# Moving zero writes, table arithmetic, one weight pass and a weight load inside an attention and mixture-of-experts kernel

## Chip, cores and metric

The kernel runs on one core of one Trainium2 chip. The metric is the device time of one execution in microseconds (us). Three runs of the kernel before took 637.21, 634.17 and 636.15 us, a median of 636.15 us. The profiled execution took 632.04 us.

## What is computed

The reference has two halves. The first is linear attention with a decay for each head, over 4 batches, 8 heads, 768 positions and a head width of 64:

```
state = gamma * state + k[t] (outer) v[t]
y[t]  = q[t] @ state / sqrt(64)          gamma[h] = 1 - 2**(-5 - h)
```

The 8 heads of a position are joined to one row of 512, which gives 3072 rows x. The second half is a mixture of 8 experts with noise on the gate:

```
l = x @ w_gate + log(1 + exp(x @ w_noise)) * noise
the two largest l of a row pick two experts; their softmax gives two weights
out[row] = sum over the two of  weight * relu(x @ w1[e]) @ w2[e]
```

w1[e] is 512 x 1024 and w2[e] is 1024 x 512.

## The kernel before, in words

**Attention.** The 3072 positions are cut into 24 chunks of 128, six for each batch. A loop over j = 0 to 23 handles one chunk a turn, written out in full (no loop on the chip). All orders inside a turn are fixed by the program text: every engine works its own instructions in that order. In turn j TensorE does the score products of chunk j + 1 (`qk`, L365), the output from within the chunk (`y_in`, L378), two tiny products for the sum of squares (`x_total`, L407), the output from the carried state (L386), the new state (L396), the transposes of chunk j - 2 (`x_rows`, L422) and its gate products (`logits`, L435 and L438). GpSimd scales the queries two chunks ahead (`q_scale`, L346) and the values one chunk ahead (`v_scale`, L340). VectorE applies the mask and splits rows into an f16 part and its remainder (`x_lo`, L416); ScalarE forms the f16 part (`x_hi`, L412), squares, copies the state and copies transposed rows out. The attention rows are written to a buffer in device memory, xbuf (`x_store`, L428).

**The SP queue.** SyncE (SP) issues nearly all plain DMAs, in program order: the loads of chunk j + 4, the row store, weight loads (`w_load`, L187), the writes of zeros to the two output tensors (`zero_out`, L307, 512 KB each), and DMA transposes (`x_t`, L705 to L709). The output must be zero before the experts' results are added to it.

**Side work in the loop.** Four tables hold what else is done in a turn: `ahead_of`, `between`, `todo` (filled by `at`) and `late`. They place the router (`route_a` to `route_f`), the preparation of expert 0's weights, and the zero writes. Weights are split into f16 parts: ScalarE forms the first (`w_hi`), then the f32 weights are scaled (`w_scaled`: L228 on GpSimd, L226 on ScalarE) and GpSimd subtracts (`w_rest`, L232).

**The table.** For each batch the router makes a product of one-hot matrices (`table`, L584) whose result LST lists, for each expert and lane, the row that it serves. `route_f` (L589, L591) adds the batches up in `acc`, a tile in SBUF. `rows_of` (L599 to L602) turns it into row numbers `idx`, replacing empty places by a padding row. With these GpSimd gathers rows by indirect DMA (`gather`, L687), and `x_t` transposes them on the way into the tile `xe`. `pR` and `pL` are two PSUM banks that the router uses as scratch.

**Experts.** Expert 0 is started while the last batch is still being routed: its products (`mm1`, L824 to L826, and `mm2`, L1001 to L1003) are cut into units that `early` places between router steps. Experts 1 to 7 run in a loop. Each has a first product `mm1s` (L900 to L902) of 28 steps; a `hook` is called after each step s and places side work. Then up to seven blocks of 128 rows follow, each a second product into one of two PSUM banks (`pO`), emptied by ScalarE (`scaled`, L971) and added to the output by indirect DMA from GpSimd (`put`, L977). Beside the blocks VectorE and ScalarE prepare the next expert: `prepare` splits its first weights, and `x_sums` (L850 to L858) reads its transposed rows `xe`. `ahead(e + 1, ...)` asks for a block's rows: a gather on GpSimd, then a transpose on SP. `w_load(e + 1, "2", ...)` loads its second weights, 2 MB in two DMAs, into the only staging tile; it waits until `w_lo` (L220) has read the old ones, the last time in step 12.

Of the kernel before, what the change touches and what calls it, by code (L numbers as in the profile page):

```python
# [40 lines left out]
NCOL = NBLK * E  # L41
# [54 lines left out]
def moe_kernel(ctx, tc, qT, kT, kt, vt, noise, wgn, w1, w2, ctab, qtab, xbuf, gbuf, out):  # L96
# [22 lines left out]
    def K(n):  # L119
        return ct[:, _C[n][0]:_C[n][1]]  # L120
# [37 lines left out]
    wide = pR[:, 144:144 + NC * NL].rearrange("p (c e) -> p c e", c=NC)  # L158
    small = pR[:, 208:208 + 48]
    second_best = pR[:, 256:256 + NC]  # L160

    def pow2(ss, target, up, down=None):

# [423 lines left out]
    def route_f(b):  # L587
        if b == 0:
            nc.vector.tensor_copy(acc, LST)  # L589
        else:  # L590
            nc.vector.tensor_tensor(acc, acc, LST, op=OP.add)  # L591

    tk = consts.tile([128, NCOL], F32, name="tk")

    def rows_of(tk, n0, n1):

        padv = work.tile([128, NCOL], F32, name="padv")
        neg = work.tile([128, NCOL], F32, name="neg")
        nc.vector.tensor_scalar(padv[:, n0:n1], tk[:, n0:n1], 0.0, K("pad"), op0=OP.is_equal, op1=OP.mult)  # L599
        nc.vector.tensor_scalar(neg[:, n0:n1], tk[:, n0:n1], 0.0, float(TOK), op0=OP.is_lt, op1=OP.mult)  # L600
        nc.vector.tensor_tensor(neg[:, n0:n1], neg[:, n0:n1], padv[:, n0:n1], op=OP.add)
        nc.vector.scalar_tensor_tensor(idx[:, n0:n1], tk[:, n0:n1], 127.0, neg[:, n0:n1], op0=OP.add, op1=OP.add)  # L602

    def ranks():

        nc.vector.tensor_copy(cum, cump)
        m = E - 2
        n, s3, s4 = R["cum"][:, 2:E], [128, m, m], [128, m, NBLK, m]
        key = hp.tile([128, m], F32, name="key")
        nc.vector.scalar_tensor_tensor(key, n, 8.0, K("tie")[:, :m], op0=OP.mult, op1=OP.add)  # L610
        cm = hp.tile(s3, F32, name="cm")
        nc.vector.tensor_tensor(cm, key[:, None, :].to_broadcast(s3), key[:, :, None].to_broadcast(s3), op=OP.is_gt)
        rk = hp.tile([128, m], F32, name="rk")
        nc.vector.tensor_reduce(rk, cm, axis=AX.X, op=OP.add)
        pm = R["pm"] = hp.tile(s3, F32, name="pm")
        nc.vector.tensor_tensor(pm, rk[:, None, :].to_broadcast(s3),
                                K("i64")[:, :m, None].to_broadcast(s3), op=OP.is_equal)
        nc.vector.tensor_tensor(cm, pm, K("lidx")[:, None, 2:E].to_broadcast(s3), op=OP.mult)
        nc.vector.tensor_reduce(rk, cm, axis=AX.X, op=OP.add)
        nc.vector.tensor_copy(eid[:, :m], rk)  # L620
        tp = hp.tile(s4, F32, name="tp")
        v = acc[:, 2 * NBLK:].rearrange("p (e t) -> p t e", e=m)
        nc.vector.tensor_tensor(tp, v[:, None].to_broadcast(s4), pm[:, :, None, :].to_broadcast(s4), op=OP.mult)
        nc.vector.tensor_reduce(tk[:, 2 * NBLK:].rearrange("p (r t) -> p r t", r=m), tp, axis=AX.X, op=OP.add)
        rows_of(tk, 2 * NBLK, NCOL)
        nc.vector.tensor_tensor(cm, pm, K("rcap")[:, 1:, None].to_broadcast(s3), op=OP.mult)
        nc.vector.memset(capd, float(CAP))
        nc.vector.tensor_reduce(capd[:, 2:E], cm.rearrange("p r e -> p e r"), axis=AX.X, op=OP.add)
# [84 lines left out]
    for b in range(B - 1):  # L713
# [9 lines left out]
            late.setdefault(n + 8, []).append((route_f, (b,)))  # L723
        if b == B0 - 1:

            late[n + 8].append((rows_of, (acc, 0, 3)))
            for t in range(3):
                ahead_of.setdefault(n + 9, []).append((gather, 0, t, 0, 128, B0 * S))
                at(n + 10, x_t, 0, t)
# [8 lines left out]
    for i in range(4):  # L738
        at(3 + i, w_load, 0, "1", i)
        at(5 + i, w_sum, 0, "1", i)  # L740
        at(10 + i, w_hi, 0, "1", i)
        between.setdefault((11, 13, 16, 18)[i], []).append((w_scaled, nc.gpsimd, 0, "1", i))
        between.setdefault((12, 14, 17, 19)[i], []).append((w_rest, 0, "1", i))
        at(8 + i, w_load, 0, "2", i)
        at(14 + i, w_sum, 0, "2", i)
        at(19 + i, w_hi, 0, "2", i)
    at(23, w_scaled, nc.scalar, 0, "2", 0)
    at(22, w_load, 1, "1", 0, 2)
    at(22, w_load, 1, "1", 2, 2)
    for i in range(8):  # L750
        at((7, 11, 12, 13, 14, 15, 16, 17)[i], zero_out, i)
    for i in range(2):
        at(10, zero_out, 12 + i)
    for j, a in ((4, (lanes16, K("lanes"))), (4, (blks16, K("blks"))), (5, (lanes.bitcast(F32), lanes16.bitcast(F32))),
# [13 lines left out]
    for j in range(NCH):  # L768
# [27 lines left out]
        y_mm(j)  # L796
        if j >= 2:
            x_rows(j - 2)
            logits(j - 2)
        slip()  # L800
        for f, a in todo.get(j, []):
            f(*a)
# [253 lines left out]
    x_rows(NCH - 1)  # L1056
    logits(NCH - 1)
    x_store(NCH - 1)
    table(b - 1)
    route_f(b - 1)  # L1060
    rows_of(acc, 3, mid + 1)
    for t in range(3, mid + 1):
        gather(0, t, 0, min(128, SECOND - t * 128), (B - 1) * S)
    for t in range(3, mid + 1):
# [32 lines left out]
    early(1)  # L1097
    table(b)
    route_f(b)
    rows_of(acc, mid, 2 * NBLK)  # L1100
    for t in range(mid, NBLK):
        gather(0, t, SECOND - t * 128 if t == mid else 0)
    for t in range(mid, NBLK):
# [91 lines left out]
    for e in range(1, E):  # L1195
        more = e + 1 < E

        def hook(s):
# [11 lines left out]
            if s == (22 if e == 1 else 11):  # L1210
                out_scale(e, 0, len(blocks(e)))
            if more:
                if 2 <= s < 9:
                    ahead(e + 1, ((6, 0, 3, 1, 4, 2, 5)[s - 2],))
                if s in (14, 16, 18, 20):
                    w_sum(e + 1, "1", s // 2 - 7)
                if s == 26:
                    w_scale(e + 1, "1")

        mm1s(e, hook)  # L1220
        for n, t in enumerate(blocks(e)):
            if more:
                if n == 0:
                    w_load(e + 1, "2", 0, 2)
                    w_load(e + 1, "2", 2, 2)
                if n < 3:
                    prepare(e + 1, n)
                if n == 2:
# [123 lines left out]
```

## Time and profile before

| what | value |
| --- | --- |
| median of three runs | 636.15 us |
| profiled execution, own time | 632.04 us |
| its span, first to last instruction | 630.3 us |
| mean granted TensorE clock | 0.996 |
| TensorE busy (matmul) | 611.6 us, 97% |
| VectorE busy | 451.2 us, 72% |
| ScalarE busy | 391.8 us, 62% |
| GpSimd busy | 395.2 us, 63% |
| moved by DMA | 112.90 MB, mean 179 GB/s |

The table is to be read by stages, since an average over the span hides where an engine stands still. Attention ends near 115 us, expert 0 is in work until about 188 us, and the loop over experts 1 to 7 runs to about 620 us. Names in the profile: PE is TensorE, PEld its weight load, DVE VectorE, ACT ScalarE, POOL GpSimd, SP SyncE; L12 is a line of the kernel. `a <- b` says that a was written from b, or that a waited for b.

### The profile page before, as it was taken

What the parts mean: (1) busy time and instruction counts of PE and PEld (TensorE: products, weight loads), DVE (VectorE), ACT (ScalarE), POOL (GpSimd) and SP (SyncE); (2) the same over time, 40 slices, a digit from 0 to 9 for tenths busy, and PEclk for the clock granted to TensorE, in tenths of its full rate; (3) what the DMA queues carried; (4) which work ended last, traced back from release to release, by engine and by line L of the source; (5) the groups of instructions that cost most, each with busy time, mean ns of one, the idle gap of its engine ahead of it and who ended that gap; (6) DMA issues with size and microseconds to landing.
All of it is one profiled execution on the core that took longest, in us unless ns stands there. A gap on an engine that the chain in (4) does not pass through costs nothing.

```text
span 630.3 us, 13242 instructions
## 1 busy us (share of the span) xinstructions
PE 611.6 (97%) x5133; PEld 384.9 (61%) x5133; DVE 451.2 (72%) x952; ACT 391.8 (62%) x655; POOL 395.2 (63%) x278
## 2 busy tenths in 40 slices
PE   8999988999999999999999999999999999999995
PEld 5899877756755545554565446544654565445784
DVE  5679888788697795579657964796579557957720
ACT  4788877944456856586558655865586558556311
POOL 2657889525776885863687558657845674574154
PEclk9999999999999999999999999999999999999998
DMA  9999999867972597479546974787499549642043
GB/s 332 350 404 405 355 384 317 244 222 208 195 193 36 85 258 226 55 133 243 161 49 118 197 229 56 169 201 176 46 146 216 160 54 162 192 52 35 9 52 44
DMA packets 104321, 112.90 MB, mean 179 GB/s; under 512 B 64512, under 2 KB 78080, under 8 KB 100672
## 3 DMA queue, kind: packets, MB, share of 16 engines
q1 hardware_dynamic: 83296, 84.70, 45.5%
q0 software_dynamic: 20528, 26.90, 27.3%
q8 instruction: 41, 0.67, 0.4%
q10 hardware_dynamic: 432, 0.43, 0.2%
q14 instruction: 24, 0.20, 0.1%
HBM read 72.16 MB, written 26.47 MB: 156 GB/s over the span
## 4 chain that ended last, share of the span: by engine, by line
PE 83%; DVE 8%; DMA 3%; ACT 2%; issue 1%; POOL 1%; SPq 1%; POOLq 0%; ACTq 0%; DVEq 0%
PE pO L1001 11%; PE pO L1002 11%; PE pO L1003 11%; PE pH L900 11%; PE pH L902 10%; PE pH L901 10%; PE pA L365 2%; DVE am L372 2%; PE pY L378 2%; PE pO L992 2%; PE pT L1016 2%; PE pO L990 1%; PE pO L991 1%; PE pH L824 1%; DMA in_q<-qT 1%; PE pH L826 1%
## 5 line engine op out<-in xcount | busy, mean ns | idle before, releaser
L977 POOL DMA_INDIRECT out<-ot,idx x108 | 196.1, 1816 | 139.3 <-ACT ot L971 47.8
L1002 PE MATMUL pO<-w2l,h 128*128 128x512 f16 x336 | 127.3, 379 | 0.0
L1003 PE MATMUL pO<-w2h,h 128*128 128x512 f16 x336 | 127.3, 379 | 0.0
L1001 PE MATMUL pO<-w2h,h 128*128 128x512 f16 x336 | 127.3, 379 | 0.0
L924 DVE TENSOR_TENSOR s<-pH,s 128x416 f32<-128x416 f32 (+2 forms) x84 | 47.3, 571 | 45.0 <-PE pH L902 36.7
L697 POOL DMA_INDIRECT gx<-gbuf,idx x54 | 60.9, 1128 | 28.1 <-issue 14.5
L687 POOL DMA_INDIRECT xg<-xbuf,idx x55 | 59.2, 1076 | 20.6 <-issue 15.1
L971 ACT ACTIVATE ot<-pO,gse 128x512 f32<-128x512 f32 (+2 forms) x48 | 32.7, 683 | 59.5 <-PE pO L1003 55.9
L191 ACT ACTIVATE junk<-wst 128x1024 bf16<-128x1024 f32 x64 | 67.8, 1060 | 2.9 <-DMA wst<-w 2.8
L920 ACT ACTIVATE s<-pH 128x416 f32<-128x416 f32 (+2 forms) x84 | 40.2, 508 | 30.7 <-PE pH L902 30.6
L916 ACT ACTIVATE h<-s 128x832 f16<-128x832 f32 (+2 forms) x42 | 35.9, 871 | 35.1 <-DVE s L924 35.1
L1003 PEld LDWEIGHTS <-h 128*128 128x128 f16 x336 | 32.9, 98 | 39.7
L1001 PEld LDWEIGHTS <-h 128*128 128x128 f16 x336 | 33.0, 98 | 38.8
L1002 PEld LDWEIGHTS <-h 128*128 128x128 f16 x336 | 32.9, 98 | 38.8
L902 PE MATMUL pH<-xt,wsl 128*128 128x416 f16 (+2 forms) x168 | 56.0, 333 | 0.0
L901 PE MATMUL pH<-xt,wsh 128*128 128x416 f16 (+2 forms) x168 | 56.0, 333 | 0.0
L900 PE MATMUL pH<-xt,wsh 128*128 128x416 f16 (+2 forms) x168 | 56.0, 333 | 0.0
L220 DVE SCALAR_TENSOR_TENSOR w2l<-wst,wsc,w2h 128x1024 f16<-128x1024 f32 x28 | 35.9, 1281 | 14.1 <-ACT w2h L215 14.1
L346 POOL TENSOR_TENSOR qs<-in_q,gq 128x512 f32<-128x512 f32 x21 | 26.7, 1273 | 26.3 <-DMA in_q<-qT 17.2
L917 DVE SCALAR_TENSOR_TENSOR h<-s,h 128x832 f16<-128x832 f32 (+2 forms) x42 | 41.0, 990 | 2.7 <-ACT h L916 2.7
L858 ACT ACTIVATE xt<-s 128x832 f16<-128x832 f32 (+2 forms) x28 | 24.4, 874 | 25.1 <-DVE s L857 24.9
L900 PE MATMUL pH<-xe,w1h 128*128 128x416 f16 (+2 forms) x112 | 37.3, 333 | 0.1
(217 smaller groups left out, 1477.7 us busy)
## 6 DMA issues: line engine op xcount, KB each, us to landing
wst<-w SPq DMA_DIRECT2D x28, 1024.0 KB, 7.9
in_q<-qT SPq DMA_DIRECT2D x24, 256.0 KB, 5.7
in_k<-kT SPq DMA_DIRECT2D x24, 256.0 KB, 6.4
in_v<-vt SPq DMA_DIRECT2D x24, 256.0 KB, 5.7
xbuf<-xr SPq DMA_DIRECT2D x24, 256.0 KB, 5.6
out<-zero SPq DMA_DIRECT2D x12, 512.0 KB
in_kt<-kt SPq DMA_DIRECT2D x20, 256.0 KB, 4.5
wst<-w SPq DMA_DIRECT2D x8, 512.0 KB, 6.4
```

Of the source, the lines that this page charges most:

```text
L191: nc.scalar.activation(junk, st[:, i * 1024:(i + 1) * 1024], AF.Square, accum_out=ss[:, i:i + 1])
L687: nc.gpsimd.indirect_dma_start(out=x[:p1], out_offset=None, in_=xbuf[:128 + rows], in_offset=bass.IndirectOffsetOnAxis(ap=idx[:p1, i:i + 1 ...
L697: nc.gpsimd.indirect_dma_start(out=GX[e][:, t, :], out_offset=None, in_=gbuf[:128 + rows], in_offset=bass.IndirectOffsetOnAxis(ap=idx[:, i ...
L900: nc.tensor.matmul(p, wh, bh[:, k, :], start=start and k == 0, stop=False, skip_group_check=True)
L901: nc.tensor.matmul(p, wh, bl[:, k, :], start=False, stop=False, skip_group_check=True)
L902: nc.tensor.matmul(p, wl, bh[:, k, :], start=False, stop=(k == 1), skip_group_check=True)
L917: wait.append(lambda: nc.vector.scalar_tensor_tensor(lo, src, 0.0, hi, op0=OP.max, op1=OP.subtract))
L924: nc.vector.tensor_tensor(s[:, u], p, s[:, u], op=OP.add)
L977: nc.gpsimd.indirect_dma_start(out=out[s], out_offset=bass.IndirectOffsetOnAxis(ap=idx[:n, i:i + 1], axis=0), in_=ot[:n, s * HD:(s + 1) * ...
L1001: nc.tensor.matmul(p, a, WT["2h"][:, f, :], start=(f == 0), stop=False)
L1002: nc.tensor.matmul(p, a, WT["2l"][:, f, :], start=False, stop=False)
L1003: nc.tensor.matmul(p, c, WT["2h"][:, f, :], start=False, stop=(f == FT - 1))
```

## The change

Six edits are made.

- The sum of `route_f` goes to a new place `accp` in the PSUM bank pR, and is copied back to `acc` twice; the pad test of `rows_of` writes to `padp` in the same bank instead of the tile padv in SBUF.
- The last of the four scaling passes over expert 0's first weights goes from GpSimd to ScalarE.
- Of eight zero writes in the attention loop (turns 7 and 11 to 17) three stay, in turns 7, 13 and 16; five are issued after the last row store.
- The gate products of chunk 0 are done in turn 3, beside those of chunk 1, instead of turn 2.
- In the loop over experts, the gathers and transposes for the next expert are placed in steps 12 to 18 of the first product instead of 2 to 8.
- The load of the next expert's second weights is placed in step 12, ahead of those gathers, instead of ahead of the first block.

```diff
--- before.py
+++ after.py
@@ -158,6 +158,8 @@
     wide = pR[:, 144:144 + NC * NL].rearrange("p (c e) -> p c e", c=NC)
     small = pR[:, 208:208 + 48]
     second_best = pR[:, 256:256 + NC]
+    accp = pR[:, 264:264 + NCOL]
+    padp = pR[:, 264 + NCOL:264 + 2 * NCOL]
 
     def pow2(ss, target, up, down=None):
 
@@ -588,17 +590,16 @@
         if b == 0:
             nc.vector.tensor_copy(acc, LST)
         else:
-            nc.vector.tensor_tensor(acc, acc, LST, op=OP.add)
+            nc.vector.tensor_tensor(accp, acc, LST, op=OP.add)
 
     tk = consts.tile([128, NCOL], F32, name="tk")
 
     def rows_of(tk, n0, n1):
 
-        padv = work.tile([128, NCOL], F32, name="padv")
         neg = work.tile([128, NCOL], F32, name="neg")
-        nc.vector.tensor_scalar(padv[:, n0:n1], tk[:, n0:n1], 0.0, K("pad"), op0=OP.is_equal, op1=OP.mult)
+        nc.vector.tensor_scalar(padp[:, n0:n1], tk[:, n0:n1], 0.0, K("pad"), op0=OP.is_equal, op1=OP.mult)
         nc.vector.tensor_scalar(neg[:, n0:n1], tk[:, n0:n1], 0.0, float(TOK), op0=OP.is_lt, op1=OP.mult)
-        nc.vector.tensor_tensor(neg[:, n0:n1], neg[:, n0:n1], padv[:, n0:n1], op=OP.add)
+        nc.vector.tensor_tensor(neg[:, n0:n1], neg[:, n0:n1], padp[:, n0:n1], op=OP.add)
         nc.vector.scalar_tensor_tensor(idx[:, n0:n1], tk[:, n0:n1], 127.0, neg[:, n0:n1], op0=OP.add, op1=OP.add)
 
     def ranks():
@@ -619,7 +620,7 @@
         nc.vector.tensor_reduce(rk, cm, axis=AX.X, op=OP.add)
         nc.vector.tensor_copy(eid[:, :m], rk)
         tp = hp.tile(s4, F32, name="tp")
-        v = acc[:, 2 * NBLK:].rearrange("p (e t) -> p t e", e=m)
+        v = accp[:, 2 * NBLK:].rearrange("p (e t) -> p t e", e=m)
         nc.vector.tensor_tensor(tp, v[:, None].to_broadcast(s4), pm[:, :, None, :].to_broadcast(s4), op=OP.mult)
         nc.vector.tensor_reduce(tk[:, 2 * NBLK:].rearrange("p (r t) -> p r t", r=m), tp, axis=AX.X, op=OP.add)
         rows_of(tk, 2 * NBLK, NCOL)
@@ -723,7 +724,8 @@
             late.setdefault(n + 8, []).append((route_f, (b,)))
         if b == B0 - 1:
 
-            late[n + 8].append((rows_of, (acc, 0, 3)))
+            late[n + 8].append((rows_of, (accp, 0, 3)))
+            between.setdefault(n + 9, []).append((nc.vector.tensor_copy, acc, accp))
             for t in range(3):
                 ahead_of.setdefault(n + 9, []).append((gather, 0, t, 0, 128, B0 * S))
                 at(n + 10, x_t, 0, t)
@@ -739,7 +741,7 @@
         at(3 + i, w_load, 0, "1", i)
         at(5 + i, w_sum, 0, "1", i)
         at(10 + i, w_hi, 0, "1", i)
-        between.setdefault((11, 13, 16, 18)[i], []).append((w_scaled, nc.gpsimd, 0, "1", i))
+        between.setdefault((11, 13, 16, 18)[i], []).append((w_scaled, nc.scalar if i == 3 else nc.gpsimd, 0, "1", i))
         between.setdefault((12, 14, 17, 19)[i], []).append((w_rest, 0, "1", i))
         at(8 + i, w_load, 0, "2", i)
         at(14 + i, w_sum, 0, "2", i)
@@ -747,8 +749,8 @@
     at(23, w_scaled, nc.scalar, 0, "2", 0)
     at(22, w_load, 1, "1", 0, 2)
     at(22, w_load, 1, "1", 2, 2)
-    for i in range(8):
-        at((7, 11, 12, 13, 14, 15, 16, 17)[i], zero_out, i)
+    for i in range(3):
+        at((7, 13, 16)[i], zero_out, i)
     for i in range(2):
         at(10, zero_out, 12 + i)
     for j, a in ((4, (lanes16, K("lanes"))), (4, (blks16, K("blks"))), (5, (lanes.bitcast(F32), lanes16.bitcast(F32))),
@@ -796,7 +798,8 @@
         y_mm(j)
         if j >= 2:
             x_rows(j - 2)
-            logits(j - 2)
+            for i in (() if j == 2 else (0, 1) if j == 3 else (j - 2,)):
+                logits(i)
         slip()
         for f, a in todo.get(j, []):
             f(*a)
@@ -1056,9 +1059,12 @@
     x_rows(NCH - 1)
     logits(NCH - 1)
     x_store(NCH - 1)
+    for i in range(3, 8):
+        zero_out(i)
     table(b - 1)
     route_f(b - 1)
-    rows_of(acc, 3, mid + 1)
+    rows_of(accp, 3, mid + 1)
+    nc.vector.tensor_copy(acc, accp)
     for t in range(3, mid + 1):
         gather(0, t, 0, min(128, SECOND - t * 128), (B - 1) * S)
     for t in range(3, mid + 1):
@@ -1097,7 +1103,7 @@
     early(1)
     table(b)
     route_f(b)
-    rows_of(acc, mid, 2 * NBLK)
+    rows_of(accp, mid, 2 * NBLK)
     for t in range(mid, NBLK):
         gather(0, t, SECOND - t * 128 if t == mid else 0)
     for t in range(mid, NBLK):
@@ -1210,8 +1216,11 @@
             if s == (22 if e == 1 else 11):
                 out_scale(e, 0, len(blocks(e)))
             if more:
-                if 2 <= s < 9:
-                    ahead(e + 1, ((6, 0, 3, 1, 4, 2, 5)[s - 2],))
+                if s == 12:
+                    w_load(e + 1, "2", 0, 2)
+                    w_load(e + 1, "2", 2, 2)
+                if 12 <= s < 19:
+                    ahead(e + 1, ((6, 0, 3, 1, 4, 2, 5)[s - 12],))
                 if s in (14, 16, 18, 20):
                     w_sum(e + 1, "1", s // 2 - 7)
                 if s == 26:
@@ -1220,9 +1229,6 @@
         mm1s(e, hook)
         for n, t in enumerate(blocks(e)):
             if more:
-                if n == 0:
-                    w_load(e + 1, "2", 0, 2)
-                    w_load(e + 1, "2", 2, 2)
                 if n < 3:
                     prepare(e + 1, n)
                 if n == 2:
```

## Rows read from the trace of the kernel before

**Rows 1.** Busy time by stage: us; busy (instructions) by engine; clock, DMA share, GB/s.
```profile
30.00:46.00 16.00, 16.00 (x309) 15.04 (x306) 11.91 (x37) 13.86 (x31) 8.46 (x8) 1.00 1.03 391
62.00:103.00 41.00, 34.81 (x668) 32.07 (x666) 35.74 (x136) 31.01 (x63) 36.06 (x25) 1.00 1.05 375
116.00:160.00 44.00, 43.28 (x336) 27.41 (x334) 34.08 (x129) 24.18 (x42) 20.82 (x15) 1.00 0.74 227
160.00:592.00 432.00, 431.93 (x2647) 235.89 (x2645) 315.02 (x452) 272.77 (x414) 279.16 (x189) 1.00 0.69 138
```

**Rows 2.** TensorE's waits (total, times, longest), and its timeline (start, us, what).
```profile
PE pA L365 <- POOL qs L346: 3.9, 6, 1.2
PE pL L407 <- DVE lg L458: 1.9, 1, 1.9
...
100.86 0.19 PE L407 MATMUL pL<-xss,oneb 128*64 128x1 bf16 x2 [1.91 <-DVE lg L458]
```

**Rows 3.** Timeline of GpSimd; in brackets the idle time before and its releaser.
```profile
81.00 1.26 POOL L346 TENSOR_TENSOR qs<-in_q,gq 128x512 f32<-128x512 f32 x1 [3.23 <-DMA in_q<-qT]
...
92.62 2.85 POOL L228 TENSOR_SCALAR wst<-wst,wsc 128x1024 f32<-128x1024 f32 x1
...
97.66 2.14 POOL L232 TENSOR_TENSOR w1l<-wst,w1h 128x1024 f16<-128x1024 f32 x1
```

**Rows 4.** Timeline of the SP queue, 73 to 74 us.
```profile
73.06 0.63 SPq L307 DMA_DIRECT2D out<-zero  x1
73.74 0.60 SPq L278 DMA_DIRECT2D in_q<-qT  x1
```

**Rows 5.** Timeline of VectorE: the pad test three times, and the router's read.
```profile
97.22 2.60 DVE L599 TENSOR_SCALAR padv<-acc,ct 128x3 f32<-128x3 f32 x1
...
100.55 0.25 DVE L458 TENSOR_TENSOR lg<-lg,pL 128x96 f32<-128x96 f32 x1
...
125.42 1.12 DVE L599 TENSOR_SCALAR padv<-acc,ct 128x2 f32<-128x2 f32 x1
...
146.03 0.23 DVE L599 TENSOR_SCALAR padv<-acc,ct 128x10 f32<-128x10 f32 x1
```

**Rows 6.** Timeline of ScalarE: the scaling pass on this engine.
```profile
116.78 1.16 ACT L226 ACTIVATE wst<-wst,wsc 128x1024 f32<-128x1024 f32 x1
```

**Rows 7.** Timelines of SP and TensorE, 125 to 151 us.
```profile
125.62 0.32 SPq L428 DMA_DIRECT2D xbuf<-xr  x1
130.59 2.55 SPq L709 DMA_TRANSPOSE xe<-xg  x2
...
150.76 0.25 PE L824 MATMUL pH<-xe,w1h 128*128 128x192 f16 x1
```

**Rows 8.** Timeline of TensorE: first gate product, and the product behind the gates.
```profile
20.58 0.19 PE L435 MATMUL pL<-wg,x 128*128 128x32 f16 x1 [0.57 <-DVE p2m L167]
...
20.87 1.16 PE L365 MATMUL pA<-qs,in_k 64*128 64x128 f32 x16
```

**Rows 9.** One expert, 334 to 373 us: VectorE, SP, ScalarE; transposes' time to landing.
```profile
334.22 1.28 DVE L220 SCALAR_TENSOR_TENSOR w2l<-wst,wsc,w2h 128x1024 f16<-128x1024 f32 x1
...
340.55 16.18 SPq L709 DMA_TRANSPOSE xe<-xg  x6
...
361.79 1.88 DVE L850 TENSOR_TENSOR s<-xe 128x800 f32<-128x800 f16 x2
...
368.46 0.67 ACT L971 ACTIVATE ot<-pO,gse 128x512 f32<-128x512 f32 x1
...
372.32 0.69 ACT L971 ACTIVATE ot<-pO,gse 128x512 f32<-128x512 f32 x1
...
DMA to landing us min/median/max: 3.9/5.2/8.4
```

**Rows 10.** The first expert of the loop: SP's last transposes, VectorE's first reader.
```profile
227.32 2.79 SPq L709 DMA_TRANSPOSE xe<-xg  x2
...
233.85 1.95 DVE L850 TENSOR_TENSOR s<-xe 128x832 f32<-128x832 f16 x2
```

## Prediction

> **What bounds the kernel now.** I read the profile in this order: the busy table by stage, TensorE's waits, the timelines of GpSimd, the SP queue and VectorE around the longest of these waits, then the expert loop.
>
> The stage table says where time can be gained at all [rows 1]. In the loop over experts (160 to 592 us) TensorE is busy 431.93 of 432.00 us at a granted clock of 1.00, its 2.4 GHz level. Whatever moves there can only cost. In the attention stage it is busy for all of 30 to 46 us, but only 34.81 of the 41 us from 62 to 103: 6.19 us of idle, the largest pool ahead of the loop. From 116 to 160 us another 0.72 us are idle.
>
> The list of TensorE's waits and its timeline name 5.8 of the 6.2 us [rows 2]: six waits of the score products (L365) for the scaled queries from GpSimd, 3.9 us together, and one of 1.91 us at 100.86, where the sum-of-squares product (L407) waits for a VectorE instruction of the router (L458). The rest lies in smaller waits.
>
> GpSimd's timeline shows two reasons for the six [rows 3]. At 81.00 it has sat idle 3.23 us for the query rows (in_q) to arrive. Later it has no gap: the weight pass L228 takes 2.85 us, L232 takes 2.14 us, and the scaled queries come late behind them. The SP queue shows a 512 KB zero write issued at 73.06, directly ahead of an in_q load at 73.74 that GpSimd gets only at about 81 [rows 4]. The DMA engines are full: share 1.05, 375 GB/s [rows 1].
>
> VectorE's timeline explains the 1.91 us [rows 5]. The tiny instruction padv (128x3) took 2.60 us. GpSimd's L232 ran from 97.66 to 99.80, and padv ended at 99.82; the second padv (1.12 us) ended at 126.54. The third, like the first in all but its ten columns, took 0.23 us. Behind the first stood the router's read of the bank that L407 must write.
>
> **The change, part by part.** The sum is made against the profiled execution: span 630.30 us, time 632.04 us, 1.74 us around the span. The median of the runs shown is 636.15 us, 4.1 us above it. I take the saving in microseconds from the median too.
>
> (a) Zero writes. Five of eight 512 KB writes leave the attention loop. That is 2.62 MB, at the 391 GB/s of the full stretch [rows 1] 6.7 us of DMA time in a stretch whose loads come late. The 3.23 us gap of GpSimd should go, since two or three of the five stood ahead of that load.
>
> (b) One weight pass. The last L228 (2.85 us, at 92.62) leaves GpSimd; ScalarE does the same pass in 1.16 us [rows 6], between two of its instructions that TensorE's next products need. ScalarE is busy 31.0 of 41 us there [rows 1], so I charge 0.3 us (0 to 1.2, the whole pass).
>
> (a) and (b) act on the same 3.9 us. If both worked fully all of it would go; if another engine is as late, none. VectorE is the likely next bound: 35.7 busy us of 41, of which 2.4 are the stretched padv. Squeezed into 36 us that is 93% busy. I take three quarters, 2.9 us (0 to 3.9).
>
> (c) Table in PSUM. The result of the pad test and the accumulated table move to a PSUM bank; a copy back of some 0.2 us follows twice, where VectorE is not late. If the padded test takes the 0.23 us of the undisturbed row, the router's last read ends 2.4 us earlier, at about 98.4, while L407 was due at 98.95 (100.86 less 1.91). The whole 1.91 us go. If the wait remains, nothing does. I take 1.9: the row of 0.23 us is the same instruction, only with GpSimd quiet. The second padv gives VectorE 0.9 us at 125.4; the blocks it serves are needed at 150.76 [rows 7], so I count nothing.
>
> The Trainium skill says why the place matters: by "SBUF — State Buffer" (Who interferes with whom), VectorE and GpSimd share one port pair as an exclusive lock, taken by tensor_scalar in a two-port mode, and by "VectorE: DVE Perf Modes" (Why PSUM operands drop a tier) an operand in PSUM rules that mode out. By that rule the saving is the full 1.9 us; the rows alone would leave it between 0 and 1.9.
>
> (d) Gate product postponed. At 20.58 TensorE waited 0.57 us for VectorE before the first gate products [rows 8]. They move one step on, where TensorE has no idle. The step that follows waits for VectorE anyway, so I expect a small cost, 0.3 us, eight matmuls' pitch (bounds: 0.6 gained, 0.3 lost).
>
> (e) Where the zeros go. They stand after the last store of the attention rows, issued at 125.62; the next SP instructions are two transposes at 130.59, whose blocks are used at 150.76 [rows 7]. Five writes need 6.7 us of DMA time, and the queue behind them also holds 2.1 MB of second weights and the gate rows. Cover is 20 us less the transposes' 2.55 us of issue and 5.2 us of landing [rows 7, 9]. Cost nothing; without cover, up to 6.7 us.
>
> (f) The loop. The gathers move from steps 2 to 8 of the 28 of the first product to 12 to 18; the second weights from after it to step 12, ahead of the transposes on SP. On GpSimd little changes: it works through its puts until then, and only one gather now stands behind the tail's puts. On SP the weight load waits for the last read of the old weights (VectorE L220, 334.22 to 335.50 in one expert), and the transposes wait behind it. There the other transposes started at 340.55, so some 5 us of the queue were empty, into which 2.1 MB (5.4 us at 391 GB/s) nearly fit [rows 9]. TensorE has no idle to win, so the gain is 0; the loss is the second rival below.
>
> Sum: -2.9 + 0.3 - 1.9 + 0.3 = -4.2 us, all in the first 116 us, and kept to the end because the loop behind is TensorE-bound. The span becomes 626.1 us, the profiled time 627.8 us, the median 636.15 - 4.2 = 631.95 us. I predict 631.9 us.
>
> **Rivals.** First: another engine takes the place of the late queries. For it speaks VectorE's 93%; against it, TensorE ran without idle from 30 to 46 us with ScalarE busy 13.9 of 16 us, fuller than it is later, and VectorE 11.9. Then only (c) or a part of it remains: -1.9 + 0.6, or 1.3 us, and 634.9 us. If the padded test waits as before, that the change does not do what it says, (a) and (b) alone give -2.3 and 633.9 us.
>
> Second, the other side: the transposes in the loop come late. One queue takes the weights first, so the transposes can move back by 5.4 us for the 2.1 MB, plus some 2.5 us for the block that used to go ahead of the others, 7.9 us. The slack in that expert [rows 9]: last issue started at about 355.5, landing 5.2 us later at 360.7, reader L850 at 361.79, so 1.1 us. A late reader holds ScalarE, which empties the product bank at 368.46 to 369.13; that bank is next written when the block before it ends, near 372.3: 3.2 us more. TensorE loses what exceeds 4.3 us, here 3.6 us. In the first expert the last issue started near 228.9, landing at 234.1 against the reader at 233.85: no slack but the 3.2 us, a loss of 4.7 us [rows 10]. Two such experts lose 8.3 us: 631.9 + 8.3 = 640.2 us. For it speaks the small slack; against it that the load can start in the empty 5 us. It decides from 4.3 us of delay on.
>
> The Trainium skill speaks against the change here: "DMA: Bandwidth & Descriptors" (Queues, rings and completion order) says that each DMA engine takes the descriptors of SP's queue in ring order. By that rule all transposes behind the weights start after them, which gives the 640.2 us if nothing of the load is over by then.
>
> Third: all 6.2 us of idle go and the 0.6 us of charges don't come. Then 636.15 - 6.2 = 629.95 us.
>
> **How the numbers follow.** Forecast (3 to 5.5 us saved) 0.55; first rival 0.28; second 0.10; third 0.07. The measurement tells no change from 0.5%, here 3.2 us. Faster by more: nine tenths of the forecast and the third rival, 0.57. Same: the rest of the forecast, the first rival, and a small part of the second where its loss only eats the gain, 0.35. Slower: 0.08. The range runs from 628.5, a little below the third rival, to 637.0, which takes in the first and a loop loss up to 5 us; outside it lies most of the second. The likeliest case's own range is 630.5 to 633.2 us.
>
> **What would show it.** Right: idle of TensorE between 62 us and the end of the attention stage falls from 6.2 to under 2.5 us; padv near 0.2 us at its first place; no wait of L407 for L458; GpSimd's waits for in_q shorter after 70 us; the first expert product some 4 us earlier. Wrong in (a) and (b): the L365 waits stay, or the same time turns up as waits of L378 for VectorE. Wrong in (f): any idle of TensorE from 160 to 592 us, next to VectorE waits for xe. The prediction fails if the attention stage gains under 2 us or the loop loses over 2 us.

## The result, and the profile after

The changed kernel takes 630.53 us (median of six runs, 629.08 to 632.73) against 636.89 us for the kernel before on the same chip: a ratio of 0.9909 [0.9880, 0.9937] (the 95% interval in brackets, here and below), 5.8 us less (4.0 to 7.6). Forecast were 631.9 us and 4.2 us less. The time came as predicted; the terms of the sum did not. Ratios, and the savings worked out from them, are of fast runs alone; medians are of all runs, and on the first chip below a few of these were slow, so a ratio there is not quite the quotient of the medians.

The two profiled executions differ by far less: 630.65 us after (span 628.8 us) against 632.04 us before. The profiled execution of before lies below every timed run of that kernel (634.17 to 638.64 on the chip of the result). So its trace is a poor yardstick for the saving, and what made it short turns out to bear on the whole case.

Busy time by stage after (us; busy with instructions for TensorE, its weight load, VectorE, ScalarE, GpSimd; clock, DMA share, GB/s), against [rows 1]:

```profile
62.00:103.00 41.00, 37.27 (x704) 34.44 (x704) 36.44 (x157) 34.59 (x70) 37.18 (x28) 1.00 1.03 346
...
160.00:592.00 432.00, 430.39 (x2645) 235.63 (x2644) 313.57 (x449) 271.84 (x412) 281.19 (x187) 1.00 0.66 138
```

From 62 to 103 us TensorE idles 3.73 us where it idled 6.19. From 160 to 592 us it idles 1.61 us where it idled 0.07. TensorE's timeline shows the places (start, duration, what; in brackets the idle time before and its releaser), against [rows 2]; the single line below the block is the first expert product of the kernel before:

```profile
86.39 1.16 PE L367 MATMUL pA<-qs,in_k 64*128 64x128 f32 x16 [1.16 <-POOL qs L348]
90.72 1.16 PE L367 MATMUL pA<-qs,in_k 64*128 64x128 f32 x16 [0.67 <-POOL qs L348]
97.76 0.19 PE L409 MATMUL pL<-xss,oneb 128*64 128x1 bf16 x2 [0.27 <-ACT w2h L217]
...
112.53 0.32 PE L827 MATMUL pH<-xe,w1h 128*128 128x384 f16 x1 [0.50 <-DMA xe<-xg]
...
191.14 0.34 PE L903 MATMUL pH<-xt,wsh 128*128 128x416 f16 x1 [1.50 <-ACT s L923]
```
```profile
115.74 0.32 PE L824 MATMUL pH<-xe,w1h 128*128 128x384 f16 x1 [0.69 <-DMA xe<-xg]
```

(Lines of the changed kernel are two or three higher: L365 is now L367, L407 is L409, L824 is L827, L900 is L903.) The wait of the sum-of-squares product is 0.27 us in place of 1.91. The late queries are hardly better, 3.2 us in five waits against 3.9 in six. The first expert product starts at 112.53, 3.2 us earlier than before's 115.74, and 1.5 us of that are lost at 191.14.

VectorE's timeline after, against [rows 5], and GpSimd's, against [rows 3]:

```profile
96.25 0.23 DVE L600 TENSOR_SCALAR pR<-pR,ct 128x3 f32<-128x3 f32 x1
...
96.70 0.16 DVE L602 TENSOR_TENSOR neg<-neg,pR 128x3 f32<-128x3 f32 x1
...
97.45 0.25 DVE L460 TENSOR_TENSOR lg<-lg,pL 128x96 f32<-128x96 f32 x1
```
```profile
80.01 1.27 POOL L348 TENSOR_TENSOR qs<-in_q,gq 128x512 f32<-128x512 f32 x1 [2.68 <-PE pY L388]
...
94.06 2.14 POOL L234 TENSOR_TENSOR w1l<-wst,w1h 128x1024 f16<-128x1024 f32 x1
96.15 1.28 POOL L348 TENSOR_TENSOR qs<-in_q,gq 128x512 f32<-128x512 f32 x1
...
144.63 1.08 POOL L698 DMA_INDIRECT gx<-gbuf,idx  x1 [16.84 <-DMA gbuf<-gateb]
```

The pad test (L600 now) takes 0.23 us. GpSimd works on qs from 96.15 to 97.43, right over the pad test and the three small VectorE instructions behind it (L601 to L603, the last ends at 97.05), and none of them is held. The gap ahead of 80.01 is still 2.68 us.

The SP queue after, against [rows 4, 7]:

```profile
71.47 1.24 SPq L309 DMA_DIRECT2D out<-zero  x1
72.77 0.60 SPq L280 DMA_DIRECT2D in_q<-qT  x1
...
123.08 5.63 SPq L309 DMA_DIRECT2D out<-zero  x5
128.97 4.73 SPq L710 DMA_TRANSPOSE xe<-xg  x2
...
136.07 0.38 SPq L536 DMA_DIRECT2D gbuf<-gateb  x1
```

A zero write still stands directly ahead of a query load, at 71.47 and 72.77: it is one of the three that stay. That load lands 7.1 us later, at about 79.9, and GpSimd starts at 80.01. So the 2.68 us end with the load, though the profile names another releaser.

### The profile page after: what moved, and what is told of

Same layout as the page of the kernel before. It is cut to its first block, busy times and chain, and to the rows that moved or that the text cites. A ratio compares the mean times of both kernels' runs of the same rounds, so it can differ in the third digit from the quotient of the medians.

```text
span 628.8 us, 13238 instructions
## 1 busy us (share of the span) xinstructions
PE 611.4 (97%) x5133; PEld 384.7 (61%) x5133; DVE 447.7 (71%) x954; ACT 392.5 (62%) x656; POOL 394.9 (63%) x277
## 4 chain that ended last, share of the span: by engine, by line
PE 77%; DVE 7%; DMA 7%; ACT 3%; SPq 3%; issue 2%; POOL 1%; POOLq 0%; DVEq 0%; ACTq 0%
PE pH L903 11%; PE pO L1004 10%; PE pO L1005 10%; PE pO L1006 10%; PE pH L905 10%; PE pH L904 10%; SPq L710 3%; DMA xbuf<-xr 2%; DMA xe<-xg 2%; PE pO L995 2%; PE pA L367 2%; PE pO L994 2%; PE pO L993 2%; DMA in_q<-qT 1%; PE pY L380 1%
## 5 line engine op out<-in xcount | busy, mean ns | idle before, releaser
L980 POOL DMA_INDIRECT out<-ot,idx x108 | 198.6, 1839 | 104.2 <-ACT ot L996 33.0
L688 POOL DMA_INDIRECT xg<-xbuf,idx x55 | 55.9, 1016 | 50.3 <-DMA xe<-xg 35.7
L698 POOL DMA_INDIRECT gx<-gbuf,idx x54 | 64.1, 1188 | 32.8 <-DMA gbuf<-gateb 16.8
L903 PE MATMUL pH<-xt,wsh 128*128 128x416 f16 (+2 forms) x168 | 56.0, 333 | 1.5 <-ACT s L923 1.5
L903 PE MATMUL pH<-xe,w1h 128*128 128x416 f16 (+2 forms) x112 | 37.3, 333 | 0.1
```

Of the source, the lines that this page charges most:

```text
L688: nc.gpsimd.indirect_dma_start(out=x[:p1], out_offset=None, in_=xbuf[:128 + rows], in_offset=bass.IndirectOffsetOnAxis(ap=idx[:p1, i:i + 1 ...
L698: nc.gpsimd.indirect_dma_start(out=GX[e][:, t, :], out_offset=None, in_=gbuf[:128 + rows], in_offset=bass.IndirectOffsetOnAxis(ap=idx[:, i ...
L903: nc.tensor.matmul(p, wh, bh[:, k, :], start=start and k == 0, stop=False, skip_group_check=True)
L980: nc.gpsimd.indirect_dma_start(out=out[s], out_offset=bass.IndirectOffsetOnAxis(ap=idx[:n, i:i + 1], axis=0), in_=ot[:n, s * HD:(s + 1) * ...
```

## Experiments

Twelve runs of nine kernels (the kernel before and the changed one among them) were made on three chips. The kernel before took 650.09 us on the first, 635.89 on the second and 636.74 on the third (medians), and every ratio is to runs of before on the same chip.

### First chip: both halves, and where the zeros stand

**The kernel before once more**, unchanged.

> The kernel before, unchanged, for a second trace: the profiled execution before was 632.04 us where the median of six runs is 636.89. Theory A (the gain lies in attention, and the traced execution was a lucky one there): ratio 1.000, the second trace has more TensorE idle than 6.2 us between 62 and 103 us, and its loop over experts again has under 0.2 us of idle. Theory B (the loop is what typical executions lose): the second trace shows 1 us or more of TensorE idle between 160 and 592 us, beside VectorE waits for xe. If it comes out at 632 us again, the 4.8 us belong to neither and the traces are as good as they are.

Measured: 648.61 us, 0.9994 [0.9955, 1.0033]. In its trace TensorE idles 6.84 us from 62 to 103 us, as theory A has it, but also 4.75 us from 195 to 592 us, which theory A rules out.

**The four edits ahead of the loop**, the loop as before (lines against the changed kernel):

```
-                if 12 <= s < 19:
+                if 2 <= s < 9:                 # and w_load(e + 1, "2") back in block 0
```

> Only the four edits ahead of the expert loop: table in PSUM, one weight pass on ScalarE, five zero writes behind the last row store, gate products of chunk 0 one turn later; the loop as before. Theory A: nearly the whole of the change's ratio of 0.991, so 0.990 to 0.994, 630 to 633 us. Theory B: most of the gain is missing, 0.996 to 1.000, and the trace has idle TensorE in the loop. In both the trace should show the same late start of expert 1 as the changed kernel (one wait of about 1.5 us near 190 us).

Measured: 648.61 us, 0.9966 [0.9927, 1.0004], by its ratio in theory B's range, though the runs of this kernel spread from 640.72 to 651.93 us.

**The two loop edits alone** (the other part of the diff):

> Only the two edits in the loop over experts: second weights asked for in step 12, gathers and transposes in steps 12 to 18; all before the loop as in the kernel before. Theory A: 0.999 to 1.001, 636 to 637.5 us, TensorE without idle in the loop in both. Theory B: 0.992 to 0.996, 632 to 634 us. The rival on the other side (transposes late behind the weights): 1.005 to 1.013, with TensorE idle beside VectorE waits for xe.

Measured: 648.83 us, 0.9996 [0.9969, 1.0024], theory A's range.

**All six edits, with the five zeros behind the gate rows:**

```
-    for i in range(3, 8):                      # behind the last row store
-        zero_out(i)
...
-    for i in range(8, 12):
+    for i in range(3, 12):                     # behind the gate rows
         zero_out(i)
```

> The changed kernel with the five moved zero writes one place further on: not ahead of the last transposes and weight load of expert 1, but behind the gate rows, together with the four writes that stand there. If the zeros ahead of the gate rows are what gives back 1.5 us of the attention gain (GpSimd waits for the gate rows until 144.6 us, its gathers and the transposes for expert 1 come out as late as before, TensorE idles 1.5 us near 190 us), that wait goes: span 1 to 1.5 us below the changed kernel's, 0.988 to 0.990. If the gate rows wait for something else: no difference from the changed kernel, 0.991. If the nine zero writes in a row now delay the transposes at 150 us: slower than the changed kernel by up to 3 us.

Measured: 640.62 us, 0.9876 [0.9828, 0.9924]. Neither theory had this: the halves gave 2.2 and 0.3 us, and the whole with one more move 8 us. Why stays open. This chip is slower in a way of its own. In the trace of before run again, TensorE also idles in the loop, and the list of waits from 195 to 592 us shows engines that wait for nothing the profile shows ("issue"), which the trace that stands ahead of the prediction does not have there on VectorE or ScalarE (columns: total, times, longest):

```profile
DVE w2l L220 <- issue: 4.0, 2, 2.1
...
ACT s L920 <- issue: 3.9, 4, 1.5
...
PE pO L1003 <- DVE h L917: 2.3, 5, 0.6
PE pO L1001 <- ACT h L916: 2.1, 3, 1.1
```

So I took the remaining questions to other chips.

### Second chip: single edits, and the zeros' place again

**The changed kernel itself:**

> The changed kernel once more, all six edits. On the last chip the four edits ahead of the loop alone gave 0.9966 and the two in the loop alone 0.9996; the version with all six and five zero writes further back gave 0.9876. If the edits add up (theory A), this kernel lies at 0.993 to 0.997 of before and the later zeros are what the rest came from. If the two halves need each other (theory B: the attention brings the loop forward, and only the loop edits keep what was won), it lies at 0.986 to 0.991, beside the version with later zeros.

Measured: 631.60 us, 0.9926 [0.9900, 0.9952], between the ranges of the two theories.

**The version with late zeros:**

> The six edits, with the five zero writes behind the gate rows. Theory A (zeros ahead of the transposes delay expert 1's rows): 3 to 5 us below the kernel with all edits as they stand, because transposes, weights and gate rows of SP come 5.6 us earlier; GpSimd's wait for the gate buffer, 16.84 us in the changed kernel's trace, falls to about 11. Theory B (the halves need each other and the zeros' place is worth little): within 1.5 us of the kernel with all edits.

Measured: 633.55 us, 0.9947 [0.9925, 0.9970]. The gates arrive earlier, GpSimd's gather of them starts at 141.17 against 145.40 in the changed kernel here, and yet nothing is gained: the median is 1.95 us above that of the changed kernel, and the intervals overlap. The 0.9876 was not repeated; the 3 to 5 us that my theory A gave to the place of the zeros did not come.

**Table and pad test in PSUM alone** (acc becomes accp, padv becomes padp, nothing else):

> Only the table and the pad test moved to PSUM, nothing else. Theory A: the VectorE stall goes in attention (the padded test at 0.2 us in place of 2.6, no TensorE wait of about 2 to 4 us at L407's line), 0.995 to 0.998 of before. Theory B: the time given back is lost again at the first expert, 0.998 to 1.001.

Measured: 634.87 us, 0.9988 [0.9968, 1.0007], in theory B's range.

**Five zero writes moved behind the last row store, alone:**

```
-    for i in range(8):
-        at((7, 11, 12, 13, 14, 15, 16, 17)[i], zero_out, i)
+    for i in range(3):
+        at((7, 13, 16)[i], zero_out, i)
...
+    for i in range(3, 8):
+        zero_out(i)
```

> Only the zero writes moved: five of them leave the attention loop and stand behind its last row store. By the prediction's steps the attention gains up to 2.9 us (GpSimd's 3.2 us gap for its operand goes) and the place behind the row stores costs nothing: 0.995 to 0.999. Theory A on the zeros' place: the gain is given back where the rows of expert 1 come later, since nothing else starts earlier and SP has five transfers of 1.1 us more ahead of the transposes: 0.999 to 1.003.

Measured: 633.59 us, 0.9961 [0.9943, 0.9979], in the range of the prediction's steps.

The PSUM edit does what it should and gains next to nothing. In its trace the wait of L409 is gone, but TensorE stands at two later places, the second 2.99 us long, for the first expert's rows, and behind it the granted clock is 0.50 and 0.73 (120 to 124 us). This execution took 637.48 us, 2.6 us above the median of its kernel, so it shows more loss than the typical one:

```profile
108.97 1.16 PE L367 MATMUL pA<-qs,in_k 64*128 64x128 f32 x16 [1.57 <-POOL qs L348]
119.36 0.32 PE L826 MATMUL pH<-xe,w1h 128*128 128x384 f16 x1 [2.99 <-DMA xe<-xg]
```

The zeros' trace has the late VectorE in full. TensorE first, then VectorE, then GpSimd in the same microseconds, then the granted clock (last columns but two) behind the wait:

```profile
100.50 0.19 PE L407 MATMUL pL<-xss,oneb 128*64 128x1 bf16 x2 [3.67 <-DVE lg L458]
```
```profile
95.54 2.17 DVE L600 TENSOR_SCALAR neg<-acc 128x3 f32<-128x3 f32 x1
97.75 1.18 DVE L601 TENSOR_TENSOR neg<-neg,padv 128x3 f32<-128x3 f32 x1
98.96 0.96 DVE L602 SCALAR_TENSOR_TENSOR idx<-acc,neg 128x3 int32<-128x3 f32 x1
```
```profile
95.56 2.12 POOL L232 TENSOR_TENSOR w1l<-wst,w1h 128x1024 f16<-128x1024 f32 x1
97.65 1.25 POOL L346 TENSOR_TENSOR qs<-in_q,gq 128x512 f32<-128x512 f32 x1
98.87 1.03 POOL L340 TENSOR_TENSOR vp<-in_v,ct 128x512 f32<-128x512 f32 x1
```
```profile
100.00:102.00 2.00, 1.50 (x22) 0.75 0.06 17
102.00:104.00 2.00, 2.00 (x34) 0.50 0.65 176
```

Each of these small VectorE instructions (0.15 us elsewhere) ends within 0.1 us of the end of a GpSimd instruction: 97.71 beside 97.68, 98.93 beside 98.90, 99.92 beside 99.90. GpSimd has no gap, so VectorE is held three times running, and TensorE waits 3.67 us, not the 1.91 of [rows 2]. In the trace of before the pad test alone was held; GpSimd then stood 0.33 us for in_q, and VectorE's chain ran through:

```profile
100.13 1.29 POOL L346 TENSOR_TENSOR qs<-in_q,gq 128x512 f32<-128x512 f32 x1 [0.33 <-DMA in_q<-qT]
```

Behind the long wait the granted clock falls to 0.50, the 1.2 GHz level; behind the 1.91 us of before it stayed at 1.00. Before's attention was traced four times: the three other traces (before run again, and the loop edits alone on two chips) have waits of 4.14, 3.67 and 2.66 us at L407, each with the clock down behind it. So the gap goes with the short execution. How much of its 4.9 us below the median it explains is not shown, as the timed runs have no trace, but their mean granted clock is on record: 0.993 over the 17 runs of before on the third chip and 0.997 over the six with (a) and (b).

### Third chip: the halves, and the edits added one by one

**The four edits ahead of the loop:**

> The four edits ahead of the loop, on another chip. The changed kernel gave 0.9909 and 0.9926 of before, the zero writes alone 0.9961, PSUM alone 0.9988. Theory A (all of the gain lies ahead of the loop, as the prediction has it, and the loop edits are worth nothing): 0.991 to 0.9935. Theory B (the loop edits are needed to keep it): 0.995 to 0.998.

Measured: 631.00 us, 0.9919 [0.9888, 0.9949], theory A's range here.

**The two loop edits:**

> The two loop edits alone. Theory A: 0.999 to 1.001. Theory B: 0.996 to 0.998, TensorE idle between 195 and 592 us lower than before's.

Measured: 636.41 us, 1.0015 [0.9988, 1.0041], next to theory A.

**Zero writes and weight pass, steps (a) and (b)** (the zeros' diff above, and this line):

```
-        between.setdefault((11, 13, 16, 18)[i], []).append((w_scaled, nc.gpsimd, 0, "1", i))
+        between.setdefault((11, 13, 16, 18)[i], []).append((w_scaled, nc.scalar if i == 3 else nc.gpsimd, 0, "1", i))
```

> Zero writes and the one weight pass on ScalarE: steps (a) and (b) of the prediction, which put -2.9 us on them together (0 to -3.9, ratio 0.9954). Zero writes alone gave 0.9961, so the pass adds -0.5 us or less if the late queries have one cause that either edit removes; with two causes that add, 0.993 to 0.995.

Measured: 630.04 us, 0.9898 [0.9867, 0.9929], a larger saving than either expectation.

**Steps (a), (b) and (c)**, the PSUM edit added to that:

> Steps (a), (b) and (c): zero writes, weight pass and table in PSUM. The prediction puts -4.8 us on the three (0.9924), before the postponed gate product's +0.3. If the parts add as they stood alone on the last chip (0.9961 and 0.9988) it is 0.993 to 0.995; if the loop edits are needed, it falls short of the changed kernel by 2 us or more.

Measured: 629.35 us, 0.9892 [0.9859, 0.9924], again a larger saving than expected.

So the loop edits are worth nothing that these runs can tell, and two edits, (a) and (b), give all that six do: 6.5 us here. The kernel with the loop edits has before's attention, so its trace, taken on the same chip, shows what (a) and (b) remove, with the reserve that each kernel has one trace. TensorE's waits that matter and the clock, then VectorE and GpSimd:

```profile
73.81 1.16 PE L365 MATMUL pA<-qs,in_k 64*128 64x128 f32 x16 [1.70 <-POOL qs L346]
...
98.58 1.16 PE L365 MATMUL pA<-qs,in_k 64*128 64x128 f32 x16 [0.41 <-POOL qs L346]
...
103.42 0.20 PE L407 MATMUL pL<-xss,oneb 128*64 128x1 bf16 x2 [2.66 <-DVE lg L458]
```
```profile
104.00:106.00 2.00, 2.00 (x32) 0.56 0.94 270
106.00:108.00 2.00, 2.00 (x28) 0.59 0.89 138
```
```profile
99.65 1.98 DVE L601 TENSOR_TENSOR neg<-neg,padv 128x3 f32<-128x3 f32 x1
101.66 1.19 DVE L602 SCALAR_TENSOR_TENSOR idx<-acc,neg 128x3 int32<-128x3 f32 x1
```
```profile
72.50 1.26 POOL L346 TENSOR_TENSOR qs<-in_q,gq 128x512 f32<-128x512 f32 x1 [1.73 <-DMA in_q<-qT]
...
99.48 2.13 POOL L232 TENSOR_TENSOR w1l<-wst,w1h 128x1024 f16<-128x1024 f32 x1
101.57 1.26 POOL L346 TENSOR_TENSOR qs<-in_q,gq 128x512 f32<-128x512 f32 x1
```

The kernel with (a) and (b) has, in the same places, GpSimd's wait at 80.92 as long as ever, the weight rest 4.7 us earlier, the pad test held for 2.00 us and the rest of its chain not at all, a shorter wait of L407 and the clock at 1.00:

```profile
80.92 1.26 POOL L346 TENSOR_TENSOR qs<-in_q,gq 128x512 f32<-128x512 f32 x1 [3.27 <-DMA in_q<-qT]
...
94.76 2.14 POOL L232 TENSOR_TENSOR w1l<-wst,w1h 128x1024 f16<-128x1024 f32 x1
```
```profile
97.15 2.00 DVE L599 TENSOR_SCALAR padv<-acc,ct 128x3 f32<-128x3 f32 x1
```
```profile
100.19 0.19 PE L407 MATMUL pL<-xss,oneb 128*64 128x1 bf16 x2 [1.81 <-DVE lg L458]
```
```profile
102.00:104.00 2.00, 1.96 (x37) 1.00 0.64 193
```

Its first expert product starts at 114.09, against 118.63: 4.5 us. The pieces are 1.7 us (the wait at 73.81 is gone), 0.4 us (that at 98.58), 0.85 us (2.66 to 1.81 at L407), and 1.7 us of clock (2 us at 0.56 and 2 us at 0.59 do the work of 2.3 us), 4.65 together. By cause: all waits for queries fall from 5.0 to 2.7 us, 2.3 us; the wait of L407 and the clock behind it make 2.55 us. The two add up to 4.9 us, 0.3 us over the difference. Span for span it is 4.3 us, 633.1 to 628.8; the rest of the 6.4 us between the medians is that the profiled run with the loop edits, 634.87 us, was 1.5 us below its own median and the other 0.6 us above, and no trace shows that part.

The table has one traced execution of each kernel (starts in us) beside the ratio over all its runs.

| kernel | first expert product at | expert 1 starts at | ratio |
| --- | --- | --- | --- |
| loop edits | 118.6 | 190.8 | 1.0015 |
| PSUM | 119.4 | 193.3 | 0.9988 |
| zeros | 115.7 | 187.8 | 0.9961 |
| (a), (b) | 114.1 | 186.2 | 0.9898 |
| (a), (b), (c) | 113.2 | 185.5 | 0.9892 |
| four edits | 113.7 | 186.0 | 0.9919 |
| changed (on record) | 112.5 | 184.8 | 0.9909 |
| changed (second chip) | 111.5 | 189.1 | 0.9926 |

The last row shows a second bound. The earlier attention ends, the nearer comes the landing of rows. In that execution, the one with the earliest first product, GpSimd got its gates at 145.40 after 18.60 us of waiting, and TensorE stood for rows of expert 0, and later for an h that VectorE had not written (columns: total, times, longest):

```profile
PE pO L1006 <- DVE h L831: 2.2, 1, 2.2
PE pH L827 <- DMA xe<-xg: 1.1, 1, 1.1
```

Behind the 2.2 us the granted clock is 0.50 (180 to 182 us) and 0.65 (182 to 184), which costs 1.7 us more. With the two waits that makes 5.0 of the 5.2 us by which expert 0 takes longer there (77.5 us) than in the changed kernel on record (72.3). This execution, 633.77 us, was 2.2 us above the median of its kernel.

## Why the prediction was right, point by point

**What bounds it.** Right: all of the gain lies ahead of the first expert product. The loop edits alone gave 1.0015, and what the four others gave alone, 0.9919, is what the whole gave (0.9909 on record, 0.9926 on the second chip). On the first chip the four gave only 0.9966 [0.9927, 1.0004].

**(a) and (b), 2.9 us (0 to 3.9).** Too small, and out of its bounds: 6.5 us (4.5 to 8.5). Two things failed. The mechanism named for (a) did not happen: GpSimd's gap stays (2.68 us after, 3.27 us with (a) and (b)). The write at 73.06 [rows 4] that I held responsible is one that stays; that it is the cause was not tested. In the pair of traces on the third chip the gain came at another load, the 1.73 us at 72.50. And the bound of 3.9 us counted only TensorE's waits for queries. For these alone the 2.9 us were about right: they fell by 2.3 us in that pair, and over all traces they are 3.2 to 6.9 us where the zeros stand as before (five traces) and 2.1 to 4.4 where they are moved (nine). What (b) does to VectorE, and through it to L407 and the clock, was not priced: without the scaling pass at 92.62 [rows 3], the weight rest L232 (L234 in the changed kernel) runs at 94.06 and not at 97.66 and is over before the pad test begins. With (a) and (b) the pad test is then held only beside the two shorter GpSimd instructions that follow (2.00 us in that trace), then GpSimd has a gap of 0.78 us, L407 waits 1.81 us, and the clock stays up. I had read "later it has no gap" for GpSimd in the trace of before, and it had one, the 0.33 us at 100.13 that spared VectorE. Zeros alone gave 2.5 us, which leaves some 4 us for the pass, but that difference spans two chips, and the pass was never run by itself: how the 6.5 us divide between (a) and (b) is not shown.

**(c), 1.9 us.** Right in its mechanism, too large as a term: 0.8 us alone (loss of 0.4 to gain of 2.0) and 0.7 us on top of (a) and (b), neither apart from nothing. The pad test takes 0.23 us and L409's wait is 0.27. In the one trace of (c) alone, the time reappears as 1.57 us for late queries, 2.99 us for expert 0's rows and a low clock behind them; whether typical runs lose it there is not shown. After (a) and (b), the worst of the stall is already out of the way. The sum treated the terms as independent, and they act on one chain.

**How near the sum came** is in part luck. Of its terms, (a) and (b) were 3.6 us too small and (c) 1.2 us too large, and the two errors partly cancel. The charges for (b) and (d), 0.3 us each, no run told apart.

The rule quoted in the prediction from the Trainium skill, "SBUF — State Buffer" (Who interferes with whom), fits these traces and goes further than I took it: it also says that a VectorE instruction with two inputs in SBUF contends with a GpSimd instruction that reads SBUF. The trace agrees: L601, a tensor_tensor of 128x3, took 1.98 us beside L232 and L602 1.19 us beside L346, where both take 0.16 us undisturbed. Moving an operand of each to PSUM, as (c) does, freed all of them (0.16 us at 96.70 while GpSimd ran); in none of the eight traces with (c) is one of the four held.

**(d), 0.3 us.** Not settled. The four edits came out at 631.00 us and (a), (b), (c) at 629.35 on the same chip, and these intervals overlap.

**(e), nothing.** Right as far as measured. With (a) and (b) TensorE works 34.94 of the 35 us from 160 to 195, and with the zeros elsewhere the time was no better (0.9947 against 0.9926). But the cover that I named was the wrong one. I looked at the blocks used at 150.76 and not at the rows behind them: SP's transposes start at 128.97, earlier than before's 130.59, while the gates that GpSimd gathers come no earlier than before, at 144.63 (143.74 before). In the changed kernel's trace VectorE gets expert 1's rows at 174.79 after 3.32 us of waiting, and TensorE waits the 1.50 us at 191.14. What brings the rows late was not settled.

**(f), nothing, and the second rival.** Right, and the rival did not come. TensorE is busy 396.89 of 397 us from 195 to 592. In the expert of [rows 9] SP and VectorE now show:

```profile
334.13 0.86 SPq L189 DMA_DIRECT2D wst<-w  x2
335.10 2.02 SPq L706 DMA_TRANSPOSE xe<-xg  x1
337.18 1.28 SPq L708 DMA_TRANSPOSE xe<-xg  x1
338.56 15.79 SPq L710 DMA_TRANSPOSE xe<-xg  x6
```
```profile
360.40 1.89 DVE L853 TENSOR_TENSOR s<-xe 128x800 f32<-128x800 f16 x2
```

The six transposes start at 338.56 and end at 354.35, against 340.55 and 356.73. The weights cost SP 0.86 us of issue. The second half of the load, issued at 334.7, lands 11.0 us later, at 345.7. By the rule of the Trainium skill weighed here, "DMA: Bandwidth & Descriptors" (Queues, rings and completion order), transposes behind the weights start after them, and the trace fits it: the first of the six, issued at 338.56, lands 9.0 us later, at 347.6, behind the load. The other five are issued from 346.6 on, when the load is gone, and land after 3.1 to 4.6 us (four of them are on record); the last, issued at 353.1, lands at about 357.1, and VectorE reads at 360.40. What the rival had wrong is the step from the first transpose to the last: it moved the last by up to 7.9 us, and its issue came 2.4 us earlier than before (355.5). Its landing time of 5.2 us [rows 9], too, is the median of all 50 transposes of the program and not of that expert; the same median is 4.3 us after the change.

**The first rival** (another engine becomes the bound, 634.9 us) did not come; **the third** (all 6.2 us go) is near the time of the best versions, 629.35 and 630.04 us, but not by its mechanism: 3.2 us of late queries remain after the change, with three scaling passes still on GpSimd.

**The signs named.** Right: padv and L407's wait. One sign named against (a) and (b) did come in this pair of traces: the L365 waits stay (3.2 us against 3.9). Missed: idle under 2.5 us from 62 us on (it is 3.73 to 103 us), and the first product 4 us earlier in this pair of traces (3.2). GpSimd's longest wait for in_q is hardly shorter (2.68 us against 3.23). The sign against (f), idle of TensorE from 160 to 592 us next to VectorE's wait for xe, did appear, the 1.50 us at 191.14. It does not speak against (f): those rows are expert 1's, asked for ahead of the loop, and the kernel with the loop edits alone, on the third chip, has no idle from 160 to 195 us. From 195 us on, the changed kernel has 0.11 us.

## What to carry to other kernels

Compare the profiled execution with the timed runs before taking terms from it: one that is below all of them may have had luck somewhere, and the luck may be what the change is about. Price an edit on a chain of two engines by what it does to both; terms that act on one chain do not add, and a wait that is taken away alone may only move to the next transfer. Before crediting the removal of a transfer, check that it is the one directly ahead of the late load.

## What the runs showed of the hardware

A chain of four VectorE instructions on 128x3 elements, from the pad test to idx, takes 0.80 us where it is not held (96.25 to 97.05 after, with an operand of each in PSUM). In the six traces with all its operands in SBUF it took 1.7 to 4.2 us more at this place, beside a busy GpSimd. How it was held went with the gaps between GpSimd's own instructions: with a gap of 0.33 us one instruction was held (2.60 us), without one up to three in a row, or one across three of GpSimd's (4.48 us in before run again).

The granted clock fell to the 1.2 GHz level behind TensorE's waits of 2.66, 3.67 (twice) and 4.14 us at L407, for about 4 us, and not behind those of 1.81 and 1.91 us; about 1.7 us came on top of the longer ones. Elsewhere it fell behind waits of 2.20 us (the changed kernel on the second chip), 2.99 (PSUM alone) and 3.85 (the four edits on the first chip). The length of the wait is no full rule: the clock fell behind one of 1.76 us and not behind one of 2.13 (both in before run again), and in the trace of the four edits on the first chip it fell to 0.50 at 104 us behind three short waits of 0.94 us together.

One chip ran the same program 2% slower than the others, with idle time on VectorE and ScalarE that no visible event ended.
